# Attention rows written unnormalized, ScalarE applies the factors to gathered rows, closing split between the packing steps, second search issued right behind the row numbers

## The chip, the core and the metric

The kernel runs on one core of a Trainium2 chip. The metric is the device time of one execution in microseconds (us). The core has five engines that run side by side, each in its own program order: TensorE (PE in the profile, with its weight loads as PEld), VectorE (DVE), ScalarE (ACT), GpSimd (POOL) and SyncE (SP, which here only starts transfers). An engine whose next instruction waits holds up everything behind it.

## What is computed

```python
scores = q @ k.T / 8                              # 8 batches, 8 heads, 576 rows, 64 wide
scores = where(scores >= rowmax - tau, scores, -1e9)
attn   = exp(scores - rowmax); attn /= attn.sum() # 4608 rows of x = attn @ v, 512 wide
logits = x @ w_gate                               # 8 experts
# greedy: all (row, expert) pairs by falling logit; a row goes to the first
# expert that still has room, 576 rows an expert
for e in range(8):
    out[rows of e] = relu(x[rows of e] @ w1[e]) @ w2[e]   # 512 -> 1024 -> 512
```

## The kernel before

**Attention** (function `attention`) goes through 8 batches of 4 head pairs. Its output stands transposed in SBUF (`XT`, channels by rows) and is not yet divided by the row sums; `rd_calc` makes the reciprocals `RD` (one number per row and head; `rm` holds those of the last 64 rows of a batch). `xt_unit(b,c)` turns 128 rows (64 for c=4) back with four TensorE transposes (L201), and its inner `ev` brings them out of PSUM, multiplies each 64-wide head block by its reciprocal and writes the rows to DRAM (`xrows`, DMA at L215). For batches 0 and 1 VectorE multiplies on the way out of PSUM (L208). For batches 2 to 7, 30 such units in all, ScalarE copies out and GpSimd multiplies in place (L214, 24 units), or ScalarE does eight 64x64 multiplies (L212, 6 units with c=4). These 30 units run after attention proper, interleaved with the first search.

**Routing** (class `Router`). The greedy assignment is done as eight rounds. In each, a **search** of seven steps (`phase`: `step_cmp` on VectorE, nine counting matmuls at L403, `step_flag`, `step_n`) finds the level at which one expert is full. Then comes the **pick** of that expert (`pick2`, matmul at L446), the ranks (`rank1`, `rank2`), the **packing** (`pack`: matmuls at L487 and L493) that gives the row numbers `idx`, and the **closing** (`close`, VectorE only), which takes the expert and its rows out of the logits `L` so that `prep` of the next search can start. Each step goes VectorE, TensorE, VectorE, TensorE. All VectorE work of the router is recorded at line L341.

**Expert rounds** (function `moe`). A round r needs the rows of its expert: `rows` starts five indirect gathers on GpSimd (`xg`, L615), TensorE turns each tile (L625, into a PSUM pool of two buffers), ScalarE rounds it to `xh` (L628) and VectorE takes the rest `xl`. `w1_load` and `w2_load` load the expert's weights after the pick and split them into `w1h`, `w1l` (L581, L587) and `w2h`, `w2l` (L603) in the same manner. `ffn` then does layer 1 (8 blocks of 24 matmuls at L645, 192 in all, ended by `hf` L651 and `H` L652 on ScalarE) and layer 2 (five tiles, 112 matmuls at L665, each tile ended by `y` on ScalarE, L668, and a scatter on GpSimd, L672; the halves of the last 64 rows are added at L675).

**The order** of all this on each engine is made when the program is built: `run` holds a clock of planned microseconds, and every generator (`place`, `packing`, `rows`, `w1_load`, `w2_load`, `low`) yields the planned time until its next step. The next round's search, packing, gather and transposes are so laid between the matmuls of the running round. `GA` is the planned time from the gather to the first transpose, `RW` the time between tiles, `LATS` the latency planned for a search step. On the chip only the order counts: each engine takes its instructions as written.

Of the kernel before, what the change touches and what calls it, by code (L numbers as in the profile page):

```python
# [9 lines left out]
F32 = mybir.dt.float32  # L10
# [4 lines left out]
ALU = mybir.AluOpType  # L15
# [4 lines left out]
PPB=8; LTB=1; VTB=5; HOLD=1; CAPV=3.3; RATE=(2.4,2.4); NBO=2; XAC=(4,); NDEF=4; XTB=4; XTY=1.05; XT0=2.0; XRB=2  # L20


def attention(ctx, tc, qk, vl, tau, wgd, xrows, xts, Lg, nb_batches, ident, swap, R, after_first):
# [173 lines left out]
    def xt_unit(b,c):  # L197
        ps=bank_v([128,4,128])
        n=128 if c<4 else 64
        for j in range(4):  # L200
            T.transpose(ps[:n,j],XT[b][:,j,c*128:c*128+n],ident)  # L201
        if b<nb_batches-NDEF-NBO: xr=wk.tile([128,512],F32,name="xr",bufs=XRB)
        else: xr=wk.tile([128,2,S],F32,name="pp",bufs=PPB)[:,0,:512]
        def ev():
            src=RD[b][:,:,2*c:2*c+2] if c<4 else RD["m",b][0:64]
            src=src.unsqueeze(3).to_broadcast([n,4,2,64])
            xv=xr[:n].rearrange("p (j h d) -> p j h d",j=4,h=2); pv=ps[:n].rearrange("p j (h d) -> p j h d",h=2)
            if b<nb_batches-NDEF-NBO: V.tensor_tensor(xv,pv,src,op=ALU.mult)  # L208
            elif c in XAC:
                for j in range(4):  # L210
                    for h in range(2):
                        A.activation(xv[:,j,h],pv[:,j,h],AF.Copy,scale=RD[b][:n,j,2*c+h:2*c+h+1] if c<4 else RD["m",b][0:64,j,h:h+1])  # L212
            else:
                A.activation(xv,pv,AF.Copy); G.tensor_tensor(xv,xv,src,op=ALU.mult)  # L214
            nc.sync.dma_start(xrows[b*S+c*128:b*S+c*128+n,:],xr[:n])  # L215
        return ev
# [128 lines left out]
class Router:  # L345
# [154 lines left out]
    def close(s):  # L500
        V=s.V; wk=s.wk; L=s.L

        cl=wk.tile([128,8],F32,name="cl"); V.tensor_scalar(cl,s.k("w8"),s.m,-FMAX/2,op0=ALU.is_equal,op1=ALU.mult)
        V.tensor_tensor(L,L,cl.unsqueeze(1).to_broadcast([128,NC_,8]),op=ALU.add)
        u=wk.tile([128,NC_],F32,name="u"); V.tensor_scalar(u,s.sc,BIGS,-FMAX/2,op0=ALU.is_ge,op1=ALU.mult)
        u2=wk.tile([128,NC_],F32,name="u2"); V.scalar_tensor_tensor(u2,s.sc,BIGS+CAP,u,op0=ALU.is_lt,op1=ALU.mult)
        V.tensor_tensor(L,L,u2.unsqueeze(2).to_broadcast([128,NC_,8]),op=ALU.add)
    def warm(s,n):

        ps=s.ps()  # L510
        for i in range(n): s.T.matmul(ps[:,256:384],s.ones,s.tri,start=True,stop=True)
# [26 lines left out]
    def pack(s,first):  # L538
# [14 lines left out]
LATS=[0.15,0.05,0.4]+[0.6]*5; FIX=(0.125,0.2)  # L553
GA=[7.0,5.5,7.5,9.0]; HALF=1; WARM=[20,4,50]
W1Y=5.0; L2O=(0,4,1,2,3); L2Z=1; HFB=3; RW=[0.2,0.6,1.0,2.0]; LOWP=(0,1); LPF=7; LOWT=1.4; PREPW=1; WLY=(1.0,1.0)

def moe(ctx,tc,R,start,xrows,w1,w2,out,ident):
# [10 lines left out]
    def w1_load(r,s):  # L568
        while r>0 and ("w1",r-1) not in done: yield 0.5
# [7 lines left out]
        s["w1h"]=w1p.tile([128,4,F],F32R,name="w1h"); s["w1l"]=w1p.tile([128,4,F],F32R,name="w1l")  # L577
        for k in range(4):
            t=s["w1s",k]
            if r==0:  # L580
                A.activation(s["w1h"][:,k],t,AF.Copy)  # L581
                while "idx" not in s: yield 0.25
                V.tensor_tensor(s["w1l"][:,k],t,s["w1h"][:,k].bitcast(F32),op=ALU.subtract)
                yield 1.1; continue
# [6 lines left out]
        done.add(("w1",r))  # L591
    def w2_load(r,s):
# [6 lines left out]
        while ("w1",r) not in done or (r==0 and ("x",0) not in done) or (r>0 and ("l2",r-1) not in done): yield 0.5  # L599
# [9 lines left out]
    def rows(r,s):  # L609
        while r>0 and ("x",r-1) not in done: yield 0.5  # L610
        order=(4,0,1,2,3) if r<=HALF else range(5)
        for t in order:
            n=128 if t<4 else 64
            x=wk.tile([128,D],F32,name="xg",bufs=5); s["xg",t]=x
            G.indirect_dma_start(out=x[:n],out_offset=None,in_=xrows,in_offset=IOA(ap=s["idx"][:n,t:t+1],axis=0))  # L615
        s["ei2"]=wk.tile([128,1],I32,name="ei2",bufs=2); G.tensor_copy(s["ei2"],s["ei"])
        done.add(("g",r))
        yield GA[min(r,3)]
        while r>0 and ("l1",r-1) not in done: yield 0.5
        s["xh"]=wk.tile([128,4,576],F32R,name="xh"); s["xl"]=wk.tile([128,4,576],F32R,name="xl")  # L620
        for t in order:
            n=128 if t<4 else 64
            ps=pt.tile([128,4,128],F32,name="pt")
            held[0]+=0.5
            for d in range(4): T.transpose(ps[:,d,:n],s["xg",t][:n,d*128:(d+1)*128],ident[:n,:n])  # L625
            if t<4: xv=lambda n: s[n][:,:,128*t+32*(t//2):128*t+32*(t//2)+128]; pv=ps
            else: xv=lambda n: s[n].rearrange("p k (a b) -> p k a b",a=2)[:,:,:,256:288]; pv=ps[:,:,:64].rearrange("p k (a b) -> p k a b",a=2)
            A.activation(xv("xh"),pv,AF.Copy)  # L628
            yield 0.8
            V.tensor_tensor(xv("xl"),pv,xv("xh").bitcast(F32),op=ALU.subtract)  # L630
            done.add(("row",r,t))
            if t==1: done.add(("half",r))
            yield RW[min(r,3)]
        done.add(("x",r))

    def ffn(r,s):
        H=wk.tile([128,8,2*CAP],F32R,name="H")
        for f in range(8):
            ps=pf.tile([128,2,512],F32,name="pf")
            for hs in (((0,),(1,)) if r<=HALF and f==0 else ((0,1),)):  # L640
                if hs==(1,): yield None
                for k in range(4):
                    for j,(w,x) in enumerate((("w1h","xh"),("w1h","xl"),("w1l","xh"))):
                        for h in hs:
                            T.matmul(ps[:,h,:HS],s[w][:,k,f*128:(f+1)*128],s[x][:,k,h*HS:(h+1)*HS],  # L645
                                     start=(k==0 and j==0),stop=(k==3 and j==2))
                        if not (k==3 and j==2): yield 0.125*len(hs)
# [31 lines left out]
    def place():  # L679
        for r in range(8):  # L680
# [41 lines left out]
    for r in range(8):  # L722
        while not all((n,r) in done for n in ("w1","half" if r<=HALF else "x")):
            now+=0.25; run(now)
        for d in ffn(r,st[r]):
            while d is None and ("x",r) not in done:
                now+=0.25; run(now)
            if d is None: continue
# [33 lines left out]
def build(tc, qk, vl, tau, wgd, cst_d, w1, w2, out, off, nb=8):  # L762
    nc=tc.nc
    with ExitStack() as ctx:
# [3 lines left out]
        xrows=dr.tile([8*S,512],F32,name="xrows")  # L768
# [29 lines left out]
```

## Time and profile before

| | |
|---|---|
| time, median of 3 runs (range) | 1036.67 us (1036.25 to 1037.45) |
| the profiled execution's own time | 1035.21 us |
| its span | 1033.4 us |
| PE busy | 975.2 us, 94% |
| ACT busy | 640.0 us, 62% |
| granted TensorE clock, mean | 0.982 |
| the 30 late row units and the first search | about 491 to 529 us |
| first matmul of round 0, layer 1 | 547.87 us |

The profile is one traced execution. Its own time is 1.5 us under the median, 1.8 us over its span. In the lines that follow, a group row gives the busy time, the mean duration in ns and the idle time before its instructions with what ended it; a timeline row gives start, duration, engine and line; a window row gives busy time per engine, then the granted clock of TensorE as a share of full speed.

### The profile page before, as it was taken

The page shows a single profiled execution, that of the slowest core. Times are in us where ns is not written, and L with a number is a line of the kernel's source. Part 1 is how long each engine was busy: PE and PEld are TensorE (multiplying, and loading weights), DVE is VectorE, ACT ScalarE, POOL GpSimd, SP SyncE. Part 2 cuts the span into 40 slices and gives each one's busy share as a digit, 9 for nine tenths or more (in the row PEclk, how much of TensorE's full clock was granted, in tenths as well). Part 3 has the DMA queues.
Part 4 walks back from the last instruction along what each step waited for, and adds up shares of the span by engine and source line. Part 5 has one row for each costly group of instructions (what it writes and reads, how often), then busy time and mean ns, then how long its engine had stood idle before and what let it go on. Part 6 is the DMA issues. An engine that isn't in the chain of part 4 may idle for free. (4 is left out here: it accounts for less than half of the span.)

```text
span 1033.4 us, 24027 instructions
## 1 busy us (share of the span) xinstructions
PE 975.2 (94%) x9104; PEld 709.5 (69%) x9104; DVE 777.4 (75%) x2085; ACT 640.0 (62%) x1221; POOL 323.1 (31%) x485
## 2 busy tenths in 40 slices
PE   6999999999999999998658899999999999999996
PEld 3555555555555555555547779788897978889895
DVE  6999999999999999996777677757585676744230
ACT  5898888888888888886644335444352534445340
POOL 2333333333333343331653445312204031231201
PEclk9999999999999999999878999999999999999998
DMA  6322133233433222302453251504325052363101
GB/s 224 106 67 96 65 138 127 95 138 113 153 107 107 96 72 100 108 2 93 158 206 122 82 169 48 197 28 131 130 83 168 14 185 75 125 229 127 41 11 41
DMA packets 35715, 113.03 MB, mean 109 GB/s; under 512 B 4368, under 2 KB 4752, under 8 KB 35088
## 3 DMA queue, kind: packets, MB, share of 16 engines
q1 hardware_dynamic: 28496, 89.47, 24.5%
q0 software_dynamic: 5888, 18.88, 5.8%
q10 hardware_dynamic: 1216, 3.15, 0.9%
q8 instruction: 72, 1.18, 0.5%
q14 instruction: 43, 0.35, 0.1%
HBM read 89.19 MB, written 21.23 MB: 107 GB/s over the span
## 5 line engine op out<-in xcount | busy, mean ns | idle before, releaser
L75 POOL TENSOR_SCALAR nb<-nb,taub 128x1 f32<-128x1 f32 x288 | 146.8, 510 | 296.6 <-DVE z L74 256.1
L74 DVE TENSOR_SCALAR_CACHE_REDUCE z<-sc 128x576 f32<-128x576 f32 x288 | 206.0, 752 | 34.0 <-PE sc L69 32.5
L85 ACT ACTIVATE pp<-z,nb 128x576 f32<-128x576 f32 x256 | 187.3, 772 | 34.3 <-DVE z L74 32.8
L89 DVE SCALAR_TENSOR_TENSOR pp<-z,nb,pp 128x576 f32<-128x576 f32 x256 | 199.9, 813 | 0.3
L665 PE MATMUL pf<-w2h,H 128*128 128x512 f32 x576 | 196.1, 402 | 1.1 <-DVE H L341 1.1
L69 PE MATMUL sc<-qk 64*128 64x288 f32 (+1 forms) x1280 | 181.3, 428 | 6.0 <-DMA qk<-qk_dram 5.7
L144 PE MATMUL xo<-pt,vt 128*64 128x288 f32 x1024 | 151.9, 418 | 0.7 <-ACT xt L151 0.7
L113 ACT ACTIVATE pt<-tb 128x512 f32<-128x512 f32 x256 | 140.0, 593 | 13.8 <-PE tb L98 11.7
L98 PEld LDWEIGHTS tb<-ident,pp 64*128 64x128 f32 x2304 | 85.7, 139 | 72.7 <-ACT pt L113 16.8
L665 PE MATMUL pf<-w2l,H 128*128 128x512 f32 x320 | 128.2, 401 | 0.0
L672 POOL DMA_INDIRECT out_dram<-y,idx x40 | 42.0, 1050 | 266.8 <-ACT y L668 170.0
L665 PEld LDWEIGHTS pf<-w2h,H 128*128 128x128 f32 x576 | 106.4, 189 | 19.9 <-DVE H L341 1.5
L98 PE MATMUL tb<-ident,pp 64*128 64x64 f32 x2304 | 108.8, 230 | 11.4 <-ACT pt L113 6.2
L69 PEld LDWEIGHTS sc<-qk 64*128 64x128 f32 (+1 forms) x1280 | 94.3, 179 | 35.9 <-DVE pp L89 9.2
L645 PE MATMUL pf<-xh,w1h 128*128 128x288 f32 x512 | 113.3, 300 | 1.2 <-ACT xh L628 1.2
L645 PE MATMUL pf<-xh,w1l 128*128 128x288 f32 x512 | 113.6, 300 | 0.0
L645 PE MATMUL pf<-xl,w1h 128*128 128x288 f32 x512 | 112.8, 299 | 0.0
L651 ACT ACTIVATE hf<-pf 128x576 f32<-128x576 f32 x64 | 41.7, 652 | 105.0 <-PE pf L645 94.0
L144 PEld LDWEIGHTS xo<-pt,vt 128*64 128x64 f32 x1024 | 62.5, 136 | 63.6 <-issue 26.5
L668 ACT ACTIVATE y<-pf 128x512 f32<-128x512 f32 x40 | 23.9, 598 | 115.9 <-PE pf L665 105.1
L645 PEld LDWEIGHTS pf<-xh,w1h 128*128 128x128 f32 x512 | 82.8, 189 | 3.8 <-ACT xh L628 1.7
L645 PEld LDWEIGHTS pf<-xl,w1h 128*128 128x128 f32 x512 | 82.4, 189 | 0.2 <-DVE xl L341 0.2
(170 smaller groups left out, 1355.5 us busy)
## 6 DMA issues: line engine op xcount, KB each, us to landing
qk<-qk_dram SPq DMA_DIRECT2D x31, 1008.0 KB, 4.9
w2s<-w_dram SPq DMA_DIRECT2D x32, 512.0 KB, 5.9
w1s<-w_dram SPq DMA_DIRECT2D x28, 512.0 KB, 5.8
vt<-vl_dram SPq DMA_DIRECT2D x32, 320.0 KB, 5.4
xrows<-pp SPq DMA_DIRECT2D x24, 256.0 KB, 2.0
xts<-xt SPq DMA_DIRECT2D x2, 1152.0 KB, 5.3
pt<-xts SPq DMA_DIRECT2D x2, 1152.0 KB, 6.8
xrows<-xr SPq DMA_DIRECT2D x8, 256.0 KB, 2.0
```

The source lines that it names most:

```text
L69: T.matmul(sc[o,f,:HS], kd["q",h][r,c], kd[k,h][r,:],start=True,stop=True)
L74: V.tensor_scalar(z,SC.pop(t)[:,:,:HS],-0.125,None,op0=ALU.mult,op1=ALU.min,accum_out=nb[:,0:1])
L75: G.tensor_scalar(nb[:,1:2],nb[:,0:1],taub[:,0:1],None,op0=ALU.add)
L85: A.activation(pview(t),ZB[t].rearrange("p a b -> p (a b)"),AF.Exp,bias=NBI[t][:,0:1],scale=-1.0)
L89: V.scalar_tensor_tensor(pv,ZB.pop(t).rearrange("p a b -> p (a b)"),NBI[t][:,1:2],pv,op0=ALU.is_le,op1=ALU.mult,accum_out=den_of(p)[:,p%4, ...
L98: g=slice(64*r,64*r+64); T.transpose(o[:,r],x[g],ident[g,g])
L113: A.activation(PT[p][:,i%2,:,(i//2)*128:(i//2+1)*128].rearrange("p k (r q) -> p r k q",r=2),tb,AF.Copy)
L144: T.matmul(xo[64*h:64*h+64,:HS],v[:,u,64*h:64*h+64],PT[p][:,h,u,q],start=(u==0),stop=False,skip_group_check=True)
L645: T.matmul(ps[:,h,:HS],s[w][:,k,f*128:(f+1)*128],s[x][:,k,h*HS:(h+1)*HS], start=(k==0 and j==0),stop=(k==3 and j==2))
L651: A.activation(hf,ps[:,:,:HS],AF.Relu)
L665: T.matmul(ps[:,0,:],H[:,f,c:c+128],s[w][:,f],start=(f==0 and j==0),stop=e)
L672: G.indirect_dma_start(out=out,out_offset=IOA(ap=s["idx"][:n,t:t+1],axis=0),in_=y[:n],in_offset=None)
```

## The change

1. `xt_unit` no longer multiplies. The row tile is 520 wide (`XW`): 512 unnormalized values and the row's 8 reciprocals. VectorE copies (batches 0 and 1, the 8 factors by GpSimd), or ScalarE copies both (the 30 late units: one 128x512 and one 128x8 activation each). Rows in `xrows` are 2080 instead of 2048 bytes.
2. In `rows`, a new `scale(t)` multiplies the gathered tile by its factors before it is turned: eight ScalarE activations for a tile in rounds 2 to 7, for three of five tiles in round 1 and for one in round 0; one VectorE multiply for the others.
3. `close` is split into `close1` and `close2`, which in round 0 stand between the packing steps; the second search is issued at once behind the row numbers. Round 0's `w1l` is made in column pieces in front of the layer-1 blocks that need them, and round 0 takes its layer-1 matmuls in another order.
4. `GA`, `RW` and `LATS` have other numbers.

How the order moves: three places at the end of round 0's layer 2. On **ScalarE**, `w1h` and `xh` are those of round 1, and `y` is round 0's output tile. Before:

```order
L628 ACTIVATE xh<-pt 128x8x32
L628 ACTIVATE xh<-pt 128x4x128
L668 ACTIVATE y<-pf 128x512
L587 ACTIVATE w1h<-w1s 128x512
L628 ACTIVATE xh<-pt 128x4x128
L587 ACTIVATE w1h<-w1s 128x512
L628 ACTIVATE xh<-pt 128x4x128 x2
L587 ACTIVATE w1h<-w1s 128x512
L668 ACTIVATE y<-pf 128x512 x2
```

After (the first row is the eviction of the last layer-2 tile):

```order
L708 ACTIVATE y<-pf 128x512
L596 ACTIVATE w1h<-w1s 128x512
L632 ACTIVATE xg<-xg 64x64 x8
L650 ACTIVATE xh<-pt 128x8x32
L650 ACTIVATE xh<-pt 128x4x128
L632 ACTIVATE xg<-xg 128x64 x8
L596 ACTIVATE w1h<-w1s 128x512
L650 ACTIVATE xh<-pt 128x4x128
L596 ACTIVATE w1h<-w1s 128x512
L650 ACTIVATE xh<-pt 128x4x128
L632 ACTIVATE xg<-xg 128x64 x8
L650 ACTIVATE xh<-pt 128x4x128
```

All five `xh` stood ahead of the last two evictions; now they stand behind the last one, with three groups of eight multiplies among them.

On **TensorE**, L649 (before: L625) are the transposes of round 1's rows. Before, with layer 2 on both sides of each:

```order
L665 MATMUL pf<-w2l,H 128x512
L625 MATMUL pt<-ident,xg 128x64 x4
L665 MATMUL pf<-w2h,H 128x512 x2
L665 MATMUL pf<-w2l,H 128x512
L409 MATMUL rps<-cn,eyer 32x8 x4
L625 MATMUL pt<-ident,xg 128x128 x4
L665 MATMUL pf<-w2h,H 128x512 x2
L665 MATMUL pf<-w2l,H 128x512
```

After, from the last layer-2 matmuls to the first of round 1's layer 1 (nine counting matmuls of the search left out at the dots):

```order
L705 MATMUL pf<-w2l,H 128x512
L705 MATMUL pf<-w2h,H 128x512
L649 MATMUL pt<-ident,xg 128x64 x4
...
L649 MATMUL pt<-ident,xg 128x128 x8
L406 MATMUL rps<-cn,e_543 32x8 x4
L649 MATMUL pt<-ident,xg 128x128 x8
L686 MATMUL pf<-xh,w1h 128x288
L686 MATMUL pf<-xl,w1h 128x288
```

All five tiles are turned behind layer 2's last matmul and ahead of layer 1's first.

On **GpSimd**, before, the gathers `xg` of round 1 stand behind one scatter of round 0; after, they stand behind four scatters and the addition `y5`. The table counts the same for every round: how many of the next round's five tiles are turned behind the last layer-2 matmul, and which ScalarE instructions stand from the last eviction `y` to the `xh` of the last tile.

| end of layer 2 of round | turned behind it, before | after | on ScalarE behind the last `y`, after |
|---|---|---|---|
| 0 | 0 | 5 | 24 multiplies, 3 `w1h`, 5 `xh` |
| 1 | 0 | 3 | 19 multiplies, 4 `w2h`, 3 `xh` |
| 2 | 0 | 2 | 10 multiplies, 2 `w2h`, 2 `xh` |
| 3 | 0 | 1 | 3 multiplies, 1 `w2h`, 1 `xh` |
| 4 | 1 | 1 | 1 multiply, 1 `xh` |
| 5 | 0 | 1 | 5 multiplies, 1 `w2h`, 1 `xh` |
| 6 | 0 | 0 | none |

The pick of round 1's expert stood behind 186 of round 0's 192 layer-1 matmuls; it stands behind 44 of the 112 layer-2 matmuls that follow.

The diff, cut to its core:

```diff
@@ xt_unit
-        if b<nb_batches-NDEF-NBO: xr=wk.tile([128,512],F32,name="xr",bufs=XRB)
-        else: xr=wk.tile([128,2,S],F32,name="pp",bufs=PPB)[:,0,:512]
+        early=b<nb_batches-NDEF-NBO
+        if early: xr=wk.tile([128,XW],F32,name="xr",bufs=XRB)
+        else: xr=wk.tile([128,2,S],F32,name="pp",bufs=PPB)[:,0,:XW]
...
-            if b<nb_batches-NDEF-NBO: V.tensor_tensor(xv,pv,src,op=ALU.mult)
-            elif c in XAC:
...
+            if early:
+                V.tensor_copy(xv,ps[:n]); G.tensor_scalar(fv,src,1.0,0.0,op0=ALU.mult,op1=ALU.add)
             else:
-                A.activation(xv,pv,AF.Copy); G.tensor_tensor(xv,xv,src,op=ALU.mult)
+                A.activation(xv,ps[:n],AF.Copy); A.activation(fv,src,AF.Copy)
@@ pack
-        if first: s.warm(WARM[0])
+        if first: s.warm(WARM[0]); s.close1()
...
-        if first: s.warm(WARM[1])
+        if first: s.warm(WARM[1]); s.close2()
@@
-LATS=[0.15,0.05,0.4]+[0.6]*5; FIX=(0.125,0.2)
-GA=[7.0,5.5,7.5,9.0]; HALF=1; WARM=[20,4,50]
+LATS=[0.15,0.2,0.4]+[0.6]*5; FIX=(0.125,0.2)
+GA=[4.5,6.5,7.0,8.0]; HALF=1; WARM=[20,4,50]
@@ w1_load, round 0
+            for a,b in ((0,1),(1,2),(2,4),(4,8)):
+                while ("row",0,1 if a==0 else 3) not in done: yield 0.1
+                o=slice(128*a,128*b)
+                for k in range(4):
+                    V.tensor_tensor(s["w1l"][:,k,o],s["w1s",k][:,o],s["w1h"][:,k,o].bitcast(F32),op=ALU.subtract)
@@ rows
+        def scale(t):
+            if r>1 or (t in (4,1,3) if r==1 else t==4):
+                x=s["xg",t][:128 if t<4 else 64]
+                for h in range(8):
+                    A.activation(x[:,64*h:64*h+64],x[:,64*h:64*h+64],AF.Copy,scale=x[:,D+h:D+h+1])
+                    if r>1: yield 0.22
+                return
...
+            V.tensor_tensor(v,v,s["xg",t][:n,D:XW].unsqueeze(2).to_broadcast([n,8,64]),op=ALU.mult)
...
+        if r==1: yield from scale(order[0])
+        for i,t in enumerate(order):
+            if r>1: yield from scale(t)
+            turn(t)
+            if r==1 and i<4: yield from scale(order[i+1])
@@ place
                 yield from packing(r,s)
-                yield 2.3; R.close(); yield 1.4
+                yield 0.1
```

More of the change, by code (lines that the diff above doesn't have):

```diff
@@ L568, in w1_load @@
     def w1_load(r,s):
-        while r>0 and ("w1",r-1) not in done: yield 0.5
+        while r>0 and ("w1a",r-1) not in done: yield 0.5
         q=nc.scalar if r==0 else nc.sync
@@ L725, in moe @@
         for d in ffn(r,st[r]):
-            while d is None and ("x",r) not in done:
-                now+=0.25; run(now)
-            if d is None: continue
+            if type(d) is tuple:
+                while d not in done:
+                    now+=0.25; run(now)
+                continue
             held[0]=0.0; now+=d; run(now); now+=held[0]; clk[0]=now
```

83 lines of the change are left out of this document (51 added, 32 removed).

## The prediction

> **What bounds the kernel now.** The page comes first: TensorE is busy for 94% of the span, and its granted clock dips only around slices 21 to 23.
>
> ```profile
> PE 975.2 (94%) x9104; PEld 709.5 (69%) x9104; DVE 777.4 (75%) x2085; ACT 640.0 (62%) x1221; POOL 323.1 (31%) x485
> PEclk9999999999999999999878999999999999999998
> ```
>
> Next the windows by stage: the 30 late row units with the first search; pick to row numbers; row numbers to layer 1; round 0's layer 1; its layer 2; and one later round. The columns are PE, PEld, DVE, ACT and POOL busy, then the clock.
>
> ```profile
> 491.00:529.00 38.00, 23.69 (x218) 18.66 (x218) 26.86 (x54) 23.89 (x72) 27.60 (x24) 0.81 0.51 178
> 529.00:537.00 8.00, 5.53 (x67) 4.95 (x68) 4.93 (x19) 1.48 (x2) 0.00 (x0) 0.62 0.68 230
> 537.00:548.00 11.00, 5.07 (x52) 3.94 (x49) 10.62 (x18) 4.33 (x6) 6.72 (x6) 0.72 0.51 164
> 548.00:585.00 37.00, 34.39 (x301) 31.89 (x302) 26.03 (x62) 15.52 (x32) 17.11 (x14) 0.94 0.17 58
> 585.00:619.00 34.00, 31.67 (x200) 23.92 (x200) 22.74 (x62) 10.51 (x20) 11.37 (x11) 1.00 0.57 187
> 681.00:740.00 59.00, 59.00 (x441) 51.35 (x440) 40.56 (x110) 25.64 (x50) 12.04 (x11) 1.00 0.33 113
> ```
>
> Two regimes stand here. From 491 to 548 nobody is full: that stretch is a chain through VectorE and TensorE. From 548 on TensorE is the bound. What TensorE waits for from layer 2 of round 0 to layer 2 of round 7, the view of waits lists whole:
>
> ```profile
> PE pf L665 <- DVE H L341: 1.1, 1, 1.1
> PE pt L625 <- DMA xg<-xrows,idx: 1.1, 3, 0.6
> PE rps L403 <- DVE cmp L341: 0.7, 2, 0.5
> PE pf L645 <- ACT xh L628: 0.5, 1, 0.5
> PE cps L487 <- DVE R L341: 0.4, 1, 0.4
> PE rps L419 <- DVE jka L341: 0.4, 1, 0.4
> PE pt L625 <- DVE xl L341: 0.2, 1, 0.2
> ```
>
> That is 4.4 us in 415. So a microsecond won in the chain of 491 to 548 is won at the end, and a microsecond in which TensorE has nothing to do after 585 is lost at the end.
>
> **Part 1, the late row units and the first search.** In this stretch small VectorE instructions take as long as the GpSimd multiply that runs beside them. The timeline of the first search, then the same instructions in the second search:
>
> ```profile
> 498.23 3.15 POOL L214 TENSOR_TENSOR pp<-pp,rd 128x512 f32<-128x512 f32 x3 [0.55 <-ACT pp L214]
> 499.37 1.04 DVE L341 TENSOR_SCALAR E<-cst,sm 128x34 f32<-128x34 f32 x1
> 500.44 0.98 DVE L341 SCALAR_TENSOR_TENSOR E<-cst,sm,E 128x34 f32<-128x34 f32 x1
> 521.83 2.25 DVE L341 TENSOR_TENSOR cmp<-b,E 128x1152 bf16<-128x1152 f32 x1
> ...
> 545.93 1.35 DVE L341 TENSOR_TENSOR cmp<-b,cst 128x1152 bf16<-128x1152 f32 x1
> 554.44 0.24 DVE L341 TENSOR_SCALAR E<-cst,sm 128x34 f32<-128x34 f32 x1
> 554.72 0.25 DVE L341 SCALAR_TENSOR_TENSOR E<-cst,sm,E 128x34 f32<-128x34 f32 x1
> ```
>
> These three alone are 2.4 us longer beside GpSimd, 0.8 each. The search has some 16 instructions of this kind; at 0.8 that would be 13 us, but GpSimd also has pauses (27.6 of 38 us busy), so I estimate 11. The change takes all 24 GpSimd multiplies out. The Trainium skill ("SBUF — State Buffer", Who interferes with whom) says that a VectorE instruction with two SBUF inputs or in a 2-port mode and a GpSimd instruction that reads SBUF exclude each other for their whole length. By that rule, the trace agrees: 1.04 against 0.24 us.
>
> What is late next: TensorE's order is the same here, and each unit's transposes wait for a PSUM buffer that ScalarE must empty. ScalarE pays, per unit, 0.60 us plus a 128x8 copy that the trace does not show; its nearest row is the 64x64 multiply, 8 in 1.69 us, so 0.2 us.
>
> ```profile
> 514.97 1.69 ACT L212 ACTIVATE pp<-xo,rm 64x64 f32<-64x64 f32 x8
> L214 ACT ACTIVATE pp<-xo 128x512 f32<-128x512 f32 x24 | 14.2, 598 | 12.7 <-PE xo L201 9.4 <-issue 1.7 <-PE sc L419 0.5
> ```
>
> 30 times 0.8 is 24 us, as busy as before (23.89) but evenly spread. ScalarE then allows a search of 26 us, VectorE's chain one of 38 − 11 = 27. The six units ahead of the first counting step wait for ScalarE and give 2 us back. I take **−9**, bounds −5 (ScalarE's copy costs twice as much) and −12 (clock at full speed throughout).
>
> **Part 2, row numbers to layer 1.** Before, this takes 547.87 − 536.76 = 11.1 us:
>
> ```profile
> 536.60 0.16 DVE L341 SCALAR_TENSOR_TENSOR idx<-cps,ih 128x5 int32<-128x5 f32 x1
> 547.87 0.61 PE L645 MATMUL pf<-xh,w1h 128*128 128x288 f32 x1 [0.69 <-ACT xh L628]
> xg<-xrows,idx POOLq DMA_INDIRECT x40, 3.7
> L341 DVE TENSOR_TENSOR w1l<-w1s,w1h 128x1024 fp32r<-128x1024 f32 x4 | 4.8, 1220 | 0.4 <-DMA w1s<-w_dram 0.3
> ```
>
> `close1` fits where VectorE waits for the packing; `close2` delays the row numbers by a few tenths. Behind them, the first gather lands as late as before (3.7 us from issue), the eight multiplies of the first tile add 1.7 us, VectorE's multiply of a 512-wide tile half of 1.22 us; against that, 4.8 us of `w1l` and the closing no longer stand ahead of `xl` on VectorE, and the first search step is done in the meantime. I take **0**, from −2 to +3. The 32 bytes more per row change nothing that a row here could price. VectorE's copies for batches 0 and 1 lie beside attention's matmuls, where TensorE is full: 0.
>
> **Part 3, the ends of layer 2.** Here the added ScalarE work meets the late second search. By the table of the order, five, three, two, one, one and one tiles are turned behind the last layer-2 matmul, and ScalarE, in order, must first evict that matmul's tile. Durations:
>
> ```profile
> L668 ACT ACTIVATE y<-pf 128x512 f32<-128x512 f32 x40 | 23.9, 598 | 115.9 <-PE pf L665 105.1 <-issue 10.7
> L587 ACT ACTIVATE w1h<-w1s 128x512 fp32r<-128x512 f32 x56 | 32.3, 621 | 3.3 <-ACT y L668 3.3
> L628 ACT ACTIVATE xh<-pt 128x512 fp32r<-128x512 f32 x32 | 19.1, 597 | 46.2 <-PE pt L625 46.1
> L628 ACT ACTIVATE xh<-pt 128x256 fp32r<-128x256 f32 x8 | 3.1, 383 | 11.5 <-PE pt L625 11.5
> 602.13 0.46 PE L625 MATMUL pt<-ident,xg 64*128 64x64 f32 x4 [0.59 <-DMA xg<-xrows,idx]
> 606.86 0.63 PE L625 MATMUL pt<-ident,xg 128*128 128x128 f32 x4
> 544.02 1.12 PE L625 MATMUL pt<-ident,xg 128*128 128x128 f32 x4 [1.82 <-DMA xg<-xrows,idx]
> 556.41 0.39 PE L403 MATMUL rps<-oh,cmp 128*128 128x32 bf16 x9
> 558.14 0.29 PE L409 MATMUL rps<-cn,e 128*32 128x8 f32 x4 [0.71 <-DVE cn L341]
> ```
>
> The multiplies of a gathered tile (128x64, from SBUF) are not in the trace; their row is again L212: 1.7 us for eight.
>
> Round 0 to 1, from the last layer-2 matmul: eviction 0.6, `w1h` 0.5, multiplies 1.7, transposes 0.5, `xh` 0.4 makes 3.7; counting and second tile 1.0, `xh` 0.6, multiplies 1.7, transposes 0.65 makes 7.6; `xh` 0.6, `w1h` 0.5, `xh` 0.6, multiplies 1.7, transposes 0.65 makes about 11.4, and only then layer 1. In that time TensorE has 3.1 us of transposes and 0.7 of counting: **7.6 idle**. The gathers may make it worse, since they now stand behind four scatters and an addition on GpSimd:
>
> ```profile
> L615 POOL DMA_INDIRECT xg<-xrows,idx x40 | 43.6, 1090 | 68.4 <-PE pf L665 35.5 <-issue 15.5 <-DMA w1s<-w_dram 9.8
> L672 POOL DMA_INDIRECT out_dram<-y,idx x40 | 42.0, 1050 | 266.8 <-ACT y L668 170.0 <-DVE ob L341 32.9 <-DVE w1l L341 29.9
> L675 POOL TENSOR_TENSOR y<-y,z 64x512 f32<-64x512 f32 x8 | 10.4, 1302 | 0.2
> ```
>
> The last two scatters and the addition are 3.4 us behind the fourth tile's eviction; I add 1.5, bounds 0 and 4.
>
> Round 1 to 2: eviction, three multiplies, `w2h` 1.7; transposes, `xh` 1.25; eight multiplies, `w2h` 2.15; transposes, `xh` 1.25; `w2h`, eight multiplies 2.2; transposes, `xh` 0.9: 9.5, of which TensorE works 2.5: **7.0 idle**. Round 2 to 3 likewise 5.3 − 1.5 = **3.8**. Rounds 3, 4 and 5: 2.2, 1.7 and 3.0 with one transpose in each: **1.7, 1.2 and 2.5**. The sum is 23.8, with the gathers 25.3. The waits that stood at these places go (1.1 for `xg`, 0.5 for `xh`): **+23.7**, from 18 to 28.
>
> Inside layer 2 the earlier tiles can hold TensorE too, where eight multiplies, an `xh` and a `w1h` (2.8 us) are more than the 10 or so matmuls between two transposes: **+2**, from 0 to 5.
>
> The clock: after the thin stretch from 537 to 548 (46% busy) the next window still has 0.94 of full speed over 37 us, which is 2.2 us of work lost. Two long idle places cost about 2 each, the third 1.5, the three short ones 0.5 each: **+7**, from 2 to 11.
>
> **Sum**: −9 + 0 + 23.7 + 2 + 7 = +23.7. On the profiled execution 1035.2 becomes 1058.9; the median of the runs stands 1.5 higher, so 1060.
>
> **Rivals.**
>
> *The ends of layer 2 are covered (faster).* What is planned late runs early on the chip: ScalarE is busy for only 25.6 of a round's 59 us. If the lists behind `y` cost less than 9 us of TensorE's time in sum, the search decides: with 5 left there, 9 won gives 1033. Against it: the list is in order behind an eviction that waits for the very matmul that ends layer 2, so free time earlier does not help it; round 0 alone holds 7.6. Chance 0.09.
>
> *The clock stays low (much slower).* The row that speaks for it is 491 to 529: TensorE 62% busy, clock 0.81. If the clock falls at every end of layer 2, each costs the 2.2 us of the window from 548 to 585 again, and 0.45 for each transpose (1.12 at low clock against 0.63, first tile less): 4.4, 3.5 and 3.1 for the first three, 2.6 for each of the others, 19 instead of 7, and 1072. The Trainium skill ("TensorE: Matmul & The Clock Gate", Part 1) says that the gate knows half and full speed and decides by free-running windows of about 3.4 us; by that rule an idle place of 7 us throttles surely and one of 2 us only if it falls well. Chance 0.17.
>
> *The search is not shortened.* If the slow VectorE instructions come from elsewhere, or ScalarE's small copies take GpSimd's place as the pace, the −9 goes: 1069. For it: ScalarE was as busy as GpSimd there. Against it: the second search's durations. Chance 0.12.
>
> **How the numbers follow.** My forecast has 0.58; within 0.2% of before (2 us, about what a measurement of this kernel can tell from no change) 0.04, where the terms cancel. The bounds of the sum reach from 18 + 0 + 2 − 12 − 2 = 6 to 28 + 5 + 11 − 5 + 3 = 42 us, which is 1043 to 1079 and holds both slow rivals; 1042 to 1078 leaves out the faster case, the equal one and little else. Faster 0.09, same 0.04, slower 0.87.
>
> **What would show it.** Right: in 491 to 520 the 128x34 instructions of VectorE take 0.25 us and the pick comes 9 us earlier; at the end of round 0's layer 2 TensorE waits some 7 to 11 us in pieces for `xg` by ScalarE and for `xh`, then 7 at round 1's, 4 at round 2's; the clock row shows dips there that were not there before. Wrong: TensorE's waits after round 0's layer 1 stay under 10 us in sum, or the pick does not move.

## The result and the profile after

The changed kernel takes 1072.21 us (median of 4 runs, 1069.34 to 1072.98); the kernel before takes 1036.55 beside it. The ratio is 1.0338, with a 95% interval from 1.0324 to 1.0351: it is slower by 35.7 us, where 23.3 were forecast (1060 against 1036.67). The profiled execution took 1072.86 us, with a span of 1071.1, 37.7 more than before.

The same view of the page as before, from the changed kernel: the first line is busy time of each engine, the second the granted clock in 40 slices.

```profile
PE 998.4 (93%) x9104; PEld 721.3 (67%) x9104; DVE 768.2 (72%) x2103; ACT 701.1 (65%) x1481; POOL 299.1 (28%) x471
PEclk9999999999999999999889799899999999999999
```

ScalarE has 61 us more, GpSimd 24 less. The dips of the clock no longer end with slice 23. The starts of layer 1, read from the first matmul of each in the trace (us in the span), place the loss; the first two rows are the two kernels, the others are experiments that come further down.

| kernel | r0 | r1 | r2 | r3 | r4 | r5 | r6 | r7 | span |
|---|---|---|---|---|---|---|---|---|---|
| before | 547.9 | 619.2 | 681.0 | 740.4 | 800.6 | 860.7 | 919.8 | 973.2 | 1033.4 |
| after | 537.1 | 616.1 | 688.6 | 756.1 | 820.8 | 885.0 | 949.8 | 1010.5 | 1071.1 |
| after, no ScalarE multiplies (e2) | 537.0 | 610.6 | 677.4 | 742.3 | 806.2 | 867.9 | 927.8 | 982.1 | 1042.6 |
| old order, multiply straight ahead (e3) | 542.1 | 625.2 | 695.3 | 760.0 | 828.4 | 895.6 | 958.0 | 1014.5 | 1075.1 |
| old order, two tiles ahead (f4) | 538.0 | 612.8 | 677.4 | 737.2 | 798.2 | 859.4 | 919.6 | 973.1 | 1033.7 |
| old order, no multiplies at all (g0) | 536.3 | 607.8 | 669.8 | 729.4 | 790.0 | 850.3 | 909.7 | 963.3 | 1023.8 |

Up to layer 1 of round 0 the change wins 10.8 us. Then each round loses: 7.7, 10.6, 8.2, 4.5, 4.0, 5.7 and 7.4 us, 48 in sum.

**The win.** The timeline of the first search in the changed kernel, VectorE's rows that answer to those of before and the pick's counting matmul; then that matmul in the kernel before:

```profile
497.67 0.24 DVE L338 TENSOR_SCALAR E<-cst,sm 128x34 f32<-128x34 f32 x1
497.94 0.25 DVE L338 SCALAR_TENSOR_TENSOR E<-cst,sm,E 128x34 f32<-128x34 f32 x1
513.58 1.36 DVE L338 TENSOR_TENSOR cmp<-b,E 128x1152 bf16<-128x1152 f32 x1
518.22 0.18 PE L443 MATMUL rps<-c,onesb 128*128 128x8 bf16 x1 [1.00 <-DVE c L338]
```

```profile
529.12 0.19 PE L446 MATMUL rps<-c,onesb 128*128 128x8 bf16 x1 [1.96 <-DVE c L341]
```

VectorE's rows take 0.24, 0.25 and 1.36 us where before they took 1.04, 0.98 and 2.25. The pick's count stands at 518.22; before, it stood at 529.12.

**The loss.** What TensorE waits for from the end of round 0's layer 2 to layer 2 of round 7 (the view of waits, whole), and then, from the same view for PEld, what its weight loads for the transposes waited for. Here a weight load starts ahead of its matmul and takes part of the wait, so the second view shows waits that the records of matmuls hide:

```profile
PE pt L649 <- ACT xg L632: 17.3, 21, 3.1
PE rps L416 <- DVE jka L338: 3.0, 3, 2.0
PE pf L686 <- ACT xh L650: 2.4, 5, 0.5
PE pt L649 <- issue: 1.3, 1, 1.3
```

```profile
PEld pt L649 <- ACT xg L632: 36.2, 61, 3.5
PEld pt L649 <- issue: 3.6, 9, 1.3
```

In the matmuls' records 24.0 us of waits stand here against 4.4 before, 17.3 of them for ScalarE's multiplies of the gathered rows. The two views overlap in time and are not to be added. The timeline at the end of round 0's layer 2 shows how they come about:

```profile
600.34 0.60 ACT L708 ACTIVATE y<-pf 128x512 f32<-128x512 f32 x1 [4.58 <-issue]
600.84 0.62 ACT L596 ACTIVATE w1h<-w1s 128x512 fp32r<-128x512 f32 x1
602.17 2.02 ACT L632 ACTIVATE xg<-xg 64x64 f32<-64x64 f32 x8 [0.71 <-DMA xg<-xrows,idx]
602.81 1.79 PE L649 MATMUL pt<-ident,xg 64*128 64x64 f32 x4 [2.55 <-ACT xg L632]
...
608.37 2.01 ACT L632 ACTIVATE xg<-xg 128x64 f32<-128x64 f32 x8
609.00 1.91 PE L649 MATMUL pt<-ident,xg 128*128 128x128 f32 x4 [3.11 <-ACT xg L632]
```

Eviction, weight half, multiplies, transposes: the chain of the forecast. The four transposes follow the multiplies two by two and take 1.79 and 1.91 us, where before such a group took 0.46 and 0.63. Most of that counts as busy. Half the clock makes up a part: the two groups here that VectorE had scaled, with no multiplies beside them, take 1.09. Inside layer 2, at full clock, the groups of rounds 1 to 5 take from 0.60 to 1.66 us, where before they took 0.46 to 0.66; four of round 6's five take 1.3 to 2.5.

The windows of TensorE's clock, at the six ends of layer 2 (columns as in the prediction: PE, PEld, DVE, ACT, POOL, then the clock):

```profile
602.50:620.00 17.50, 11.33 (x49) 7.86 (x50) 8.67 (x21) 10.34 (x33) 3.52 (x5) 0.51 0.58 193
684.50:695.00 10.50, 8.23 (x43) 7.16 (x42) 5.47 (x12) 4.90 (x14) 1.34 (x2) 0.51 0.12 37
756.00:759.50 3.50, 3.29 (x13) 2.79 (x14) 1.40 (x3) 1.12 (x3) 0.00 (x0) 0.56 0.09 36
820.80:824.30 3.50, 3.47 (x26) 3.33 (x26) 1.72 (x4) 1.02 (x2) 0.01 (x1) 0.56 0.21 80
886.00:889.30 3.30, 3.30 (x19) 3.23 (x18) 1.02 (x5) 0.47 (x1) 0.00 (x0) 0.52 0.20 79
951.00:954.30 3.30, 3.30 (x16) 3.30 (x15) 0.54 (x1) 0.00 (x0) 2.69 (x3) 0.50 0.34 102
```

The clock is at half for some 41 us: every end of layer 2 but round 6's, which turns nothing behind it, is followed by a drop. The last four last 3.4 us each and fall near the start of the next layer 1, where TensorE is full. Those four layers are 2.0, 1.7, 1.2 and 2.0 us longer than before, about 0.5 us for each us at half clock.

### The profile page after: what moved, and what is told of

It is laid out like the page before. It is cut to its first block, busy times and chain, and to the rows that moved or that the text cites. A ratio compares the mean times of both kernels' runs of the same rounds, so it can differ in the third digit from the quotient of the medians.

```text
span 1071.1 us, 24285 instructions
## 1 busy us (share of the span) xinstructions
PE 998.4 (93%) x9104; PEld 721.3 (67%) x9104; DVE 768.2 (72%) x2103; ACT 701.1 (65%) x1481; POOL 299.1 (28%) x471
## 5 line engine op out<-in xcount | busy, mean ns | idle before, releaser
L85 ACT ACTIVATE pp<-z,nb 128x576 f32<-128x576 f32 x256 | 187.3, 772 | 34.8 <-DVE z L74 33.4
L113 ACT ACTIVATE pt<-tb 128x512 f32<-128x512 f32 x256 | 140.1, 594 | 13.8 <-PE tb L98 11.5
L705 PEld LDWEIGHTS pf<-w2h,H 128*128 128x128 f32 x576 | 107.7, 189 | 19.1
L98 PE MATMUL tb<-ident,pp 64*128 64x64 f32 x2304 | 108.9, 229 | 11.7 <-ACT pt L113 6.2
L708 ACT ACTIVATE y<-pf 128x512 f32<-128x512 f32 x40 | 23.9, 597 | 111.8 <-PE pf L705 87.8
L686 PEld LDWEIGHTS pf<-xh,w1h 128*128 128x128 f32 x512 | 85.2, 198 | 4.8 <-ACT xh L650 4.7
L686 PEld LDWEIGHTS pf<-xh,w1l 128*128 128x128 f32 x512 | 85.5, 198 | 0.8 <-issue 0.8
```

The costliest lines, as they stand in the source:

```text
L85: A.activation(pview(t),ZB[t].rearrange("p a b -> p (a b)"),AF.Exp,bias=NBI[t][:,0:1],scale=-1.0)
L98: g=slice(64*r,64*r+64); T.transpose(o[:,r],x[g],ident[g,g])
L113: A.activation(PT[p][:,i%2,:,(i//2)*128:(i//2+1)*128].rearrange("p k (r q) -> p r k q",r=2),tb,AF.Copy)
L705: T.matmul(ps[:,0,:],H[:,f,c:c+128],s[w][:,f],start=(f==0 and j==0),stop=e)
```

## The experiments

The edits are shown cut to their core; most lines that only plan time or make tiles wider are left out. Theory A after this reading: the loss is ScalarE's multiplies, which stand straight ahead of the transposes in the order, behind evictions. Its rivals are the place of the turns behind layer 2 (B) and a lack of room on VectorE for multiplies (C). A fourth (D) is about the win: that the new order shortens the search, and not the missing GpSimd multiplies. In e1, e2 and f2 TensorE's order is that of the changed kernel, matmul by matmul; in e3, f4, g0 and g1 it is that of the kernel before.

**e1: the same order, VectorE multiplies.**

```
-  A.activation(x[:,64*h:64*h+64],x[:,64*h:64*h+64],AF.Copy,scale=x[:,D+h:D+h+1])
+  nc.vector.tensor_tensor(v,v,x[:n,D:XW].unsqueeze(2).to_broadcast([n,8,64]),op=ALU.mult)
```

> The changed kernel in its own order, but every gathered tile is scaled by one VectorE multiply (0.69 us in the changed kernel's trace) in place of ScalarE's eight (2.0 us). Theory A (ScalarE's eight multiplies, in line behind the evictions, hold the transposes and set their pace): about 1035 us; transposes of a 128x128 tile take 0.65 us instead of 1.9, the idle places over 0.4 us from the end of round 0's layer 2 on fall from 22 us to under 10, and half-clock windows are left at one or two ends of six. Rival B (what costs is that tiles are turned behind the last layer-2 matmul and gathered behind scatters, whichever engine scales): 1062 us or more, idle places still near 20 us. Rival C (VectorE is the tighter engine, the multiplies delay xl and the search): 1050 us, waits for DVE xg and DVE xl in place of ACT xg.

Measured: 1055.12 us, ratio 1.0171 (1.0148 to 1.0193). 17 us come back, not 37: between A and B, and nearest to C's 1050. The weight loads for the transposes wait 6.6 us for VectorE's multiply, where 36.2 were for ScalarE's. C's sign is there in part: the transposes wait 4.7 us for `xg` by VectorE, but layer 1 only 0.8 for `xl`.

**e2: the same order, no ScalarE multiplies.**

```
-  A.activation(x[:,64*h:64*h+64],x[:,64*h:64*h+64],AF.Copy,scale=x[:,D+h:D+h+1])
+  pass
```

> The changed kernel in its own order with ScalarE's multiplies of the gathered rows left out (the output lacks these factors); VectorE still scales the tiles that it scaled. Theory A: 1033 us, since ScalarE has 72 us less in line and the transposes keep TensorE's pace; the first tile behind the end of round 0's layer 2 still waits for its gather, 2 to 4 us. Rival B (position of turns and gathers): 1062 us. What this run has above 1026 (before, less the 10.8 us that the search is shorter) is the share of the position.

Measured: 1044.55 us, ratio 1.008 (1.0062 to 1.0099). So ScalarE's multiplies cost 28 us, the larger part of the loss, and A named it; but 1044.5 is 18 above the 1026 that the search's gain would leave, so something else holds a part: the order, or the VectorE multiplies that e2 keeps for rounds 0 and 1. The two together are more than the 35.7 us, since the search gives 10.

**e3: the old order with raw rows, VectorE multiplies straight ahead of the transposes.**

```
   for t in order:
+      nc.vector.tensor_tensor(v,v,xg[:n,D:XW].unsqueeze(2).to_broadcast([n,8,64]),op=ALU.mult)
       for d in range(4): T.transpose(...)
```

> The kernel before with rows stored unnormalized with their factors, each gathered tile scaled by one VectorE multiply that the planner doesn't count, so that TensorE's order is that of before: closing and second search stand where they stood. Theory A: the search gives 9 to 11 us and the 40 multiplies of 0.69 us lie beside TensorE's work, with 1 to 3 us lost at the first tile of round 0: 1027 us. Rival C (VectorE has no room in the rounds): 1036 us or more, with waits of TensorE for xl, w1l or the search's small results of over 8 us. Rival D (the search is shortened by the new order and not by taking the GpSimd multiplies out): pick not before 527 us and 1038 us.

Measured: 1074.17 us, ratio 1.0352 (1.0321 to 1.0384): as slow as the changed kernel, with neither its order nor ScalarE's multiplies. Theory A in its first form falls. Rival D falls too: the pick stands at 517.52 us. What TensorE waits for most here, from 545 us on (`issue` stands where the profile shows nothing that was waited for), and one such place in the timeline:

```profile
PE pt L624 <- issue: 15.7, 13, 3.2
PE pt L624 <- DVE xg L621: 13.3, 12, 2.1
```

```profile
875.75 0.26 PE L406 MATMUL rps<-cn,e 128*32 128x8 f32 x4
876.05 0.15 DVE L338 TENSOR_SCALAR_CACHE_REDUCE jka<-rps 32x8 f32<-32x8 f32 x1 [0.47 <-PE rps L406]
876.14 0.68 DVE L621 TENSOR_TENSOR xg<-xg 128x512 f32<-128x512 f32 x1
876.88 0.66 PE L624 MATMUL pt<-ident,xg 128*128 128x128 f32 x4 [0.53 <-DVE xg L621]
```

The multiply does not wait for its data here. It stands in VectorE's list behind a small step of the search (`jka`), which waits for TensorE's count, and TensorE's next work waits for the multiply: a round trip in which nobody is late by itself. This made theory A': a multiply put straight ahead of its transposes costs TensorE what its engine is behind, whichever engine; a lead takes that away.

**e4: the changed kernel with normalized rows** (GpSimd multiplies back, no scaling of gathered rows).

```
-  A.activation(xv,ps[:n],AF.Copy); A.activation(fv,src,AF.Copy)
+  A.activation(xv,pv,AF.Copy); G.tensor_tensor(xv,xv,src,op=ALU.mult)
-  def scale(t): ...
+  def scale(t): return iter(())
```

> The changed kernel with rows normalized ahead of storing as before (GpSimd multiplies back, no scaling of gathered rows), its closing between the packing steps and its second search kept. Theory A: pick at 529 us as before; no ScalarE chain, so the ends of layer 2 cost little; the first layer 1 may still start a little earlier against the search, and the late turns of round 0 (at 104 to 112 of 112 matmuls) cost 4 us: 1038 us. Rival B (the move of the second search makes the ends late): 1055 us or more. Rival D: pick well before 527 us.

Measured: 1036.25 us, ratio 0.9996 (0.9982 to 1.001). The new closing and the second search behind the row numbers cost nothing by themselves, and win nothing in the search: the pick's count stands at 529.35 us, as before (529.12). The turns of round 0 stand at 104 to 112 here, against 112 for all five in the changed kernel: it is the scaling, which the planner counts, that moves them to the very end. With GpSimd's multiplies back, VectorE's rows are slow again, as its timeline of the first search shows:

```profile
499.17 0.95 DVE L341 TENSOR_SCALAR E<-cst,sm 128x34 f32<-128x34 f32 x1
500.15 0.98 DVE L341 SCALAR_TENSOR_TENSOR E<-cst,sm,E 128x34 f32<-128x34 f32 x1
```

So the shorter search comes from storing the rows unnormalized, and not from the new closing or order. GpSimd's 24 multiplies are the likeliest part of that, by VectorE's rows; ScalarE's six groups of eight left with them, and no run takes the two apart.

**f4: e3 with the multiply two tiles ahead.** TensorE's order is that of before in both.

```
+  yield GA[min(r,3)]-3.0
+  scale(order[0]); scale(order[1])
+  yield 3.0
   for i,t in enumerate(order):
-      scale(t)
       for d in range(4): T.transpose(...)
       A.activation(xv("xh"),pv,AF.Copy)
+      if i<3: scale(order[i+2])
```

> The kernel before with unnormalized rows and one uncounted VectorE multiply for each gathered tile, as in the run that took 1074 us, but the multiply stands two tiles ahead of its transposes instead of straight ahead. TensorE's order is that of before. Theory A': waits for xg (20 us, and 18 us that follow the same multiplies in the records) fall to under 8 us, 1032 us. Rival C (VectorE has no room): 1060 us or more.

Measured: 1037.62 us, ratio 1.0005 (0.9996 to 1.0015). The same 40 multiplies on the same engine cost 36.5 us less, by their place in VectorE's list alone; the order of everything else on TensorE, VectorE, ScalarE and GpSimd is the same in both. From 545 us on, TensorE's wait for them is 1.9 us where it was 13.3, and the 15.7 of `issue` at the transposes are gone. The longest waits now:

```profile
PE rps L421 <- DVE jka L338: 2.5, 2, 2.1
PE rps L400 <- DVE cmp L338: 2.2, 5, 0.7
PE pt L628 <- DVE xg L618: 1.9, 2, 1.3
PE rps L406 <- DVE cn L338: 1.9, 3, 1.0
PE pt L628 <- DVE xl L338: 1.4, 1, 1.4
```

A' holds. But 1032 was expected: the search's 10 us are won and gone again.

**f2: the changed kernel, ScalarE's multiplies one tile earlier** in rounds 2 to 7, TensorE's order unchanged.

```
+  if r>1: yield from scale(order[0])
+  if r>1: yield from scale(order[1])
   for i,t in enumerate(order):
-      if r>1: yield from scale(t)
+      if r>1 and 0<i<4: yield from scale(order[i+1])
       turn(t)
```

> The changed kernel with TensorE's order unchanged; ScalarE's eight multiplies of a tile stand one tile earlier in ScalarE's list, for rounds 2 to 7 only (behind rounds 0 and 1 the places stay as they are). Theory A': the stretched transposes (1.9 us) at the turns for rounds 2 to 7 fall to 0.65, and of the 28 us that the multiplies cost (against the kernel without them) some 15 come back: 1057 us. Rival E (ScalarE lacks throughput, 2.0 us a tile behind evictions, whatever the lead): 1068 us or more.

Measured: 1053.49 us, ratio 1.0162 (1.0145 to 1.0179): 18.7 us back, with no work taken away. The weight loads' wait for the multiplies falls from 36.2 to 11.5 us. Rival E falls for this size of lead.

**f3: the idle places filled.**

```
+  if r>0 and ("l2",r-1) in done:
+      for i in range(24 if r==1 else 12): T.matmul(ps[:,i%4,:],R.ones,R.tri,start=True,stop=True)
   for d in range(4): T.transpose(...)
```

> The changed kernel with 24 (behind round 0) or 12 (later) bf16 matmuls of 128 columns, 0.06 us each at full clock, put on TensorE ahead of the transposes of each tile that is turned behind the last layer-2 matmul; their results are overwritten. Theory F (the half-clock windows, 41 us in sum from 545 us on in the changed kernel, are set off by the idle time at these places and cost 15 us): half-clock time falls under 20 us and the kernel takes 1062 us. Rival G (the filling only takes time from the chain, clock windows come from the slow transposes inside layer 2 as well): 1072 us or more, half-clock time above 30 us.

Measured: 1065.05 us, ratio 1.0274 (1.0257 to 1.0291), 7.2 us less than the changed kernel. One row of the windows for 555 to 1010 us, of the changed kernel and of f3:

```profile
555.00:1010.00 455.00, 426.23 (x2926) 360.64 (x2925) 269.12 (x685) 235.08 (x601) 106.13 (x105) 0.95 0.31 103
```

```profile
555.00:1010.00 455.00, 438.35 (x3187) 375.44 (x3186) 271.31 (x689) 237.56 (x606) 108.10 (x106) 0.97 0.31 104
```

The mean clock rises from 0.95 to 0.97: in the clock's records 41 us at half become 23.9. More work on TensorE made the kernel faster, so the clock's share is real: 7.4 us of span for 17.1 us, or 0.43 each, which makes 17.7 us for all 41. This is an extrapolation, and a low one if the filling itself took time; the 0.5 read from layer 1 above would make it some 20. Rival G falls. Theory F had expected a little more, under 20 us at half: the dips behind rounds 3 and 4 are gone and round 0's is 3.4 us long instead of 17.1, but those behind rounds 1, 2 and 5 are left (10.2, 6.8 and 3.4 us).

**f1: the changed kernel, VectorE two tiles ahead, turns close together.**

```
+  def scale(t): nc.vector.tensor_tensor(v,v,x[:,D:XW].unsqueeze(2).to_broadcast([n,8,64]),op=ALU.mult)
+  if r>0: yield GA[min(r,3)]-3.0; scale(order[0]); scale(order[1]); yield 3.0
   for i,t in enumerate(order):
-      if r>1: yield from scale(t)
       turn(t)
-      if r==1 and i<4: yield from scale(order[i+1])
+      if i<3: scale(order[i+2])
```

> The changed kernel with every gathered tile scaled by one VectorE multiply that is put two tiles ahead of its transposes (3 us by the plan for the first two), and that the planner doesn't count: the turns come out at 79 to 96 of 112 layer-2 matmuls in rounds 1 to 5 instead of 70 to 112. Theory A' (a multiply put straight ahead of its transposes makes TensorE wait for whatever its engine is behind; a lead takes the wait away): the search's gain stays and the rounds cost 4 to 6 us, 1026 us. Rival C (VectorE has no room for 3.5 us a round, on whichever place): 1040 us or more, with TensorE waiting for the search's results and xl instead. Rival B (round 0's end is late in any case): about 8 us at round 0's end alone, 1030 us.

Measured: 1036.29 us, ratio 1.0 (0.999 to 1.001). With the lead on VectorE, and with turns that no longer stand behind the last matmul (but for two of the five at round 0's end), the whole loss of the changed kernel is gone; this run alone does not tell the two apart. The 10 us of gain are missing again, as in f4, which is more than A' had; TensorE waits 5.5 us for `xl`, VectorE's other work.

**g0: where did the ten go?** The old order, raw rows, no multiplies at all (edit against f4).

```
   def scale(t):
-      nc.vector.tensor_tensor(v,v,xg[:n,D:XW].unsqueeze(2).to_broadcast([n,8,64]),op=ALU.mult)
+      return
```

> The kernel before with unnormalized rows stored and their multiplies left out on both sides (no GpSimd multiply ahead of storing, no scaling of gathered tiles; the output lacks the factors), TensorE's order that of before: the ceiling of what taking the GpSimd multiplies out can give. Theory H (the run with multiplies two tiles ahead on VectorE won 10 us up to round 0's layer 1 and gave them back, because 40 multiplies of 0.69 us delay VectorE's small results): 1027 us. Rival I (the 10 us are given back elsewhere, for instance in the longer gathered rows or in a search that ends no earlier for TensorE): 1034 us or more.

Measured: 1026.20 us, ratio 0.9901 (0.9886 to 0.9916). H is right, I falls: longer rows cost nothing that shows, and without the multiplies the ten are kept to the end. In the table above, f4 loses against g0 1.7 us up to layer 1 of round 0, 3.3 and 2.6 in rounds 0 and 1, 0.2 to 0.9 in each of rounds 2 to 5, and nothing in the last two. The two differ in the multiplies alone. From 545 us on, TensorE's waits for the search's small results (`cmp`, `cn` and `jka`) are 7.0 us with them and 2.6 without; for `xg` and `xl` 3.3 come on top. Why rounds 0 and 1 pay most was not tested.

**g1: the old order, ScalarE three tiles ahead in rounds 2 to 7.**

```
+  if r>1: yield GA[min(r,3)]-4.0; scale(order[0]); yield 2.0; scale(order[1]); scale(order[2]); yield 2.0
...
+  if i+3<5: scale(order[i+3])
```

> The kernel before with unnormalized rows; the tiles for rounds 0 and 1 are scaled by VectorE two tiles ahead, those for rounds 2 to 7 by ScalarE's eight multiplies, the first three tiles ahead of the first turn and then three tiles ahead each. Theory H with room on ScalarE (busy for 10.8 of 32 us in a layer 2): rounds 2 to 6 take no longer than before, 1033 us. Rival E (ScalarE's 2.0 us a tile still delays evictions, xh or w1h): 1040 us or more.

Measured: 1055.71 us, ratio 1.018 (1.0166 to 1.0194): slower, where H had hoped for 1033. Rival E names the engine, and the profile shows two ways in which a lead can be wrong. The timeline in layer 2 of round 4, then ScalarE's at round 6:

```profile
855.28 3.92 ACT L620 ACTIVATE xg<-xg 128x64 f32<-128x64 f32 x16
859.11 0.61 ACT L584 ACTIVATE w1h<-w1s 128x512 fp32r<-128x512 f32 x1
859.75 0.69 DVE L338 TENSOR_TENSOR w1l<-w1s,w1h 128x512 fp32r<-128x512 f32 x1 [3.76 <-ACT w1h L584]
860.36 0.15 DVE L338 TENSOR_SCALAR_CACHE_REDUCE jka<-rps 32x8 f32<-32x8 f32 x1
860.57 0.16 PE L421 MATMUL rps<-fla,onesb 128*128 128x1 bf16 x1 [2.23 <-DVE jka L338]
```

```profile
944.36 2.02 ACT L620 ACTIVATE xg<-xg 128x64 f32<-128x64 f32 x8 [4.84 <-DMA xg<-xrows,idx]
946.28 0.63 ACT L666 ACTIVATE hf<-pf 128x576 f32<-128x576 f32 x1
```

Sixteen multiplies in a row hold the next weight half for 3.9 us, VectorE's `w1l` waits for that half, and the search's small results stand behind `w1l`. From 545 us on TensorE waits 5.3 us for `cn`, 3.8 for `cmp` and 3.9 for `jka`. At round 6 the multiply stands ahead of its gather's data: ScalarE waits 4.84 us, and the eviction of layer 1 behind it holds TensorE for 3.6.

**g2: the new start with g1's rounds.** The edit is g1's lists in the changed kernel, with `GA=[4.5,6.5,7.5,9.0]` and `RW=[0.2,0.6,1.0,2.0]`.

> The changed kernel's order up to round 0's layer 1, the gathered tiles for rounds 0 and 1 scaled by VectorE two tiles ahead, those for rounds 2 to 7 by ScalarE three tiles ahead, and the turns of rounds 2 to 7 spaced as in the kernel before (planner's delays 7.5 and 9.0 behind the gathers, 1.0 and 2.0 between tiles). Theory A' and H: layer 2 of round 0 starts at 571 us, round 2 at 675, and from there on rounds as long as before: 1028 to 1031 us. Rival E: 1040 us or more.

Measured: 1048.93 us, ratio 1.013 (1.0112 to 1.0148). The start is as expected (layer 1 of round 2 at 673.8 us), and then waits of the same kinds as in g1 take 5.8 us for `hf` and 14 for the search's results.

**h1: f1 with the turns spaced as before.**

```
-GA=[4.5,6.5,7.0,8.0] ... RW=[0.2,0.6,0.2,0.6]
+GA=[4.5,6.5,7.5,8.0] ... RW=[0.2,0.6,1.0,2.0]
```

> The changed kernel's start, every gathered tile scaled by one VectorE multiply two tiles ahead of its transposes, and the turns of the rounds spaced by 1.8 to 2.8 us of the plan as in the kernel before, not by 0.4 to 1.4 (planner's delays 7.5 and 8.0 behind the gathers, 1.0 and 2.0 between tiles). Sum from rows: layer 1 of round 2 at 675.4 us as with the close turns, then rounds of 59.7, 61.0, 61.2, 60.2 and 53.6 us as in the old order with the lead, the last round 60.6: a span of 1031.7, 1033.5 in the median. Theory J (the close turns wait for xl, 5.5 us, and spacing takes these waits away): 1031 to 1034 us. Rival C (VectorE's 3.5 us a round set the time, wherever the turns stand): 1036 us, no difference from before.

Measured: 1037.27 us, ratio 1.0005 (0.9996 to 1.0014). Rival C's time, and theory J falls: the wait for `xl` falls from 5.5 to 1.0 us, and layer 1 of round 2 starts at 671.8 us, 3.6 earlier than in f1, but TensorE now waits 5.1 us for the search's `cmp` and the gain is gone by the end. No version that applies the factors beats the kernel before; f1, f4 and h1 equal it. What f4 lacks against g0 is the price of the multiplies on VectorE; for f1 and h1 there is no run without multiplies.

## Why the prediction was right and wrong

The direction and the range were right, and so was the mechanism in the main; the time was 12 us short. On the two profiled executions the sum has 23.7 us and the spans differ by 37.7, which is 14.0 more. Point by point:

- **The search (−9, bounds −5 and −12)**: the count of the pick stands 10.9 us earlier. The reason is shown by e4 and g0: with GpSimd's multiplies the 128x34 instruction takes 0.95 us, without them 0.24.
- **Row numbers to layer 1 (0)**: from the row numbers to layer 1 it is 11.1 us, as before, and from the pick's count 18.85, before 18.75. Right. Round 0's layer 1 itself is 3.3 us shorter: steps of the second search have moved into layer 2 (252 matmul records in layer 1 where 299 stood, and 222 in layer 2 where 204 stood).
- **The ends of layer 2 (+23.7)**: the places and their order of size are right. The matmuls' records show waits of 8.1, 4.6, 3.3, 1.4, 1.1 and 2.2 us behind rounds 0 to 5, where 9.1 (with the gathers), 7.0, 3.8, 1.7, 1.2 and 2.5 were forecast: 20.7 against 25.3. Two readings beneath were a little off: the third line of round 0's chain adds up to 11.7 and not 11.4, and eight multiplies take 2.0 us where the nearest row gave 1.7.
- **Inside layer 2 (+2, bounds 0 and 5)** was too small. In sum, 37.7 + 10.9 − 17.7 = 30.9 us are left for waits and slow transposes, where 25.7 were forecast. Of these the waits at the ends make 19.1 (20.7 less the 1.6 that stood there before), so some 12 remain for transposes that multiplies slow down, at the ends and inside, and for round 6. Round 6 alone, which turns all five tiles inside layer 2 and was given nothing, has a layer 2 of 33.4 us, where it was 28.0.
- **The clock (+7, bounds 2 and 11)** is the step that missed by most. It was priced by idle length: 2 us for a long place, 0.5 for a short one. The clock fell at all six ends, also behind rounds 3 and 4, where the matmuls' records show waits of 0.70, 0.21 and 0.52 and of 0.64 and 0.47 us, and it costs about 17.7 us by f3. This is the rival that had 0.17, at a price of 19. That its 1072 is the measured time to the microsecond is partly luck: its waits were 5 us too few, and its search and its clock each a little off the other way.
- **"The search is not shortened"** (1069) comes near the time too and is wrong: the pick moved. The time alone hardly separates these two rivals; the two lines named ahead, the pick and the clock row, do.
- **The reason behind the chain** was too narrow. It was put down to ScalarE and to turns behind the last matmul. e3 has neither (one tile of 35 is turned behind the last matmul, as before) and is as slow. What counts is that the multiply stands straight ahead of its reader in a list that is in order: f4 moves it two tiles up and wins 36.5 us, f2 moves ScalarE's one tile up in rounds 2 to 7 and wins 18.7.

What stays open: of the 18 us that e2 has above g0, the runs do not tell how much is due to the late turns, to the VectorE multiplies that e2 keeps in rounds 0 and 1, and to the clock.

## What to carry to other kernels

An operation put between a gather and its reader costs little by its length and much by its place: give it a lead of a tile or two (three at once were too many in g1), and look at what stands ahead of it in its own engine's list, and whether its data has landed by then. A small instruction on an engine that carries a chain of small results is paid for in that chain, even when the engine is a quarter idle, as VectorE is here. And where a forecast hangs on idle places on TensorE, price a short place like a long one as a possible drop of the clock: in the changed kernel all six places dropped it, whatever their length, though a wait of 3.6 us in g2 did not.

## What the runs showed of the hardware

- A drop of the clock needs no long wait. From 595 us to the last layer 2 of the changed kernel the drops begin at 602.80, 684.72, 756.40, 821.25, 886.10 and 950.96 us, whole multiples of 3.413 us apart, and each lasts one or more such steps. In the step in front of the one behind round 4, TensorE's records are busy for 67%, and two waits of 1.1 us in sum are what is missing:

```profile
882.69:886.10 3.41, 2.30 (x22) 1.59 (x21) 2.47 (x5) 2.83 (x8) 0.98 (x1) 1.00 0.17 38
```

  Nor is a long wait always enough. In g2 TensorE waits 3.62 us in one piece, across two such steps, and the clock stays full (a timeline row, then the windows of the two steps):

```profile
937.67 0.53 PE L691 MATMUL pf<-xh,w1h 128*128 128x288 f32 x2 [3.62 <-ACT hf L696]
932.50:935.90 3.40, 1.55 (x12) 1.32 (x10) 0.00 (x0) 1.35 (x6) 2.67 (x3) 1.00 0.71 184
935.90:939.30 3.40, 1.63 (x12) 1.63 (x13) 1.52 (x3) 3.37 (x12) 1.11 (x2) 1.00 0.58 180
```

  The Trainium skill ("TensorE: Matmul & The Clock Gate", Part 1) gives an idle window of about 3.4 us as what throttles. The steps of 3.4 us agree with the records. A window without any work is not what these records show in front of the drop at 886.10. What share of work keeps the clock up stays open: 67% busy did not here, and 46 and 48% did in g2.
- The Trainium skill ("Perfetto Trace Analysis", Optimizing Scalar/DVE Operations) says that breaking up an instruction may let work finish sooner where an engine causes bubbles. Here the transposes did start behind the first two of ScalarE's eight multiplies, and yet one multiply of 0.69 us on VectorE in the same place was 17 us better (e1) than eight of 0.34 us on ScalarE, 2.0 us a tile. The engine differs too, so this is no test of breaking up by itself.
- At 605.9 us the second tile's transposes are done, and ScalarE takes up its `xh` only at 607.88, after 2.85 us of idle whose releaser the profile calls only remote. It was not explained, and some 2 of the 3.11 us that TensorE then waits may hang on it.
